# Attention products in pieces of 128 and 256 columns, ordered by the kernel's own clock model

## The chip, the cores and the metric

The kernel runs on one core of a Trainium2 chip. The time is that of one execution on the device, in microseconds (us). A comparison of two kernels is made from several rounds on the same chip. The engines are named as in the profile: PE is TensorE's matmul, PEld its loading of weights, ACT is ScalarE, DVE is VectorE, POOL is GpSimd, SP is SyncE.

## The reference

Two independent results stand side by side in the output, each 2048 x 576.

The first is a long convolution of a state-space model. For each of 576 channels, a kernel of 2048 taps is summed from 128 complex exponentials and convolved with the input; the reference does it by FFT.

The second is attention with 32 query heads of 18 columns and one shared key and value head:

```python
q = (x @ wq).reshape(B, S, H, Dh).transpose(0, 2, 1, 3)    # S = 2048, H = 32, Dh = 18
k = x @ wk
v = x @ wv
scores = einsum("bhqd,bkd->bhqk", q, k) * Dh ** -0.5
o = einsum("bhqk,bkd->bhqd", softmax(scores), v)
out = o.transpose(0, 2, 1, 3).reshape(B, S, H * Dh) @ wo
```

## The kernel before

**Attention.** The queries are cut into four chunks of 512 (`c`), the heads into eight groups of four (`g`), the keys into sixteen blocks of 128 (`kb`). For one chunk, group and block there are two score tiles (`j` = 0, 1) of two heads each, so the main loop (`main`, L963) runs over 4 x 8 x 16 x 2 = 1024 items, numbered `i`. Each item goes through three stations:

- `scores` (L720): two matmuls of 512 columns in half precision give a tile of 128 keys by 2 x 512 queries in PSUM. There are three such tiles (`NS` = 3), used in turn.
- `exponentials` (L734): one ACT instruction turns the tile into a tile P in SBUF. Eight P tiles exist (`NP` = 8).
- `product` (L1003): the product of P with V. The four heads of two neighbouring items stand side by side in four column strips of TensorE, so a product takes two items. It has 512 columns and is cut into two halves of `HN` = 256 columns, each with four matmuls, one per strip; an fp32 matmul appears as two instructions in the trace, so a half is 8 matmul records. The sum over the sixteen key blocks is kept in one PSUM bank, which DVE then copies out (`gather`).

**The side work.** The same PE and DVE also do the query projections (`qproj`, tiles named q), the output projection (`outproj`, `outproj_part`, op), and the whole convolution in twelve chunks of 48 channels (class `Conv`: tables and their products kg, transforms hu, lu, hk, lk, inverse iy). They share one PSUM bank, tag `f`. Their code is written as generators that yield before each piece: kind "p" for a piece on PE, "v" for one on DVE, "w" for a wait, "b" for a change of ACT's function table.

**What sets the order.** The program is emitted once, in one order for each engine, and the engines keep that order. The class `Clock` (L99) follows the time on each engine while the program is written: `K.t` is PE's time, `K.s[...]` the moments at which the score tiles come free, `turn` (L189) a cost for changing between scores and the rest. Between each three scores stands `fill(i)` (L1033). It computes `free`, the moment from which the next three scores can go without waiting for ACT, and `late`, which is `free` plus the allowance `SLACK` (L57). As long as `left = late - K.t` allows it, pieces are handed out in this order of preference: the convolution (`conv.go`, with `left + LET`), side work that is under way (`beside(left, False)`), new side work where the plan is behind (`behind_plan`, L988), a half product if one is ripe and `left > ROOM` (L1046), any side work. `beside` (L993) asks for `left - 0.43 > 0`; where a due time is nearer than `URGENT` steps (a step is two items) it adds `OVER` to `left`. Nothing more being ready, `K.t` moves on to the next event or to `free`, and the scores follow. Outside `fill`, products are forced when the eight P tiles would run out (`while (i - NP) // 2 >= behind // 2`).

`behind` counts the halves that have been given out, `ripe` (L1026) says when the next one can go. The other constants are allowances and paces of the same model: `PACE` is read in `lags` (L1627), which nothing calls; `RATE` holds the convolution's DVE work to so many us a step (L1606), `AHEAD` (L1609) limits how far DVE's queue is filled ahead of PE, `PATIENCE` is the number of steps that a table change waits, `FIRST` the earliest time of the first input transform, `PLAN` and `START` say how many side units should be done by a step, `CLEAR` how near a convolution piece must be to hold back new side work, `FEW` and `NEW` compare the number of items not yet multiplied.

Of the kernel before, what the change touches and what calls it, by code (L numbers as in the profile page):

```python
# [23 lines left out]
NCH = 4  # L24
CT = 512
KT = [(k * 128, 128) for k in range(5)]
HN = 256
DT = KT[:4] + [(512, 64)]
MT = [(0, 126), (126, 126), (252, 126), (378, 126), (504, 72)]
QT = [(0, 128), (128, 128), (256, 128), (384, 128), (512, 64)]  # L30
# [16 lines left out]
NP = 8  # L47


RATE = 6.724  # L50
PACE = 1.7672
AHEAD = 0.484
NAUG = 5
URGENT = 8.8421
HELD = 0
PATIENCE = 1
SLACK = 0.2043  # L57
FEW = 12
NEW = 3
LET = -0.1  # L60
PLAN = 0.629
START = 6.0
OVER = 0.6
CLEAR = 1.6188

LATE = {1: [0], 3: [1], 5: [2], 6: [3]}

# [10 lines left out]

HOP = 0.075
GRAIN = 128  # L80
FIRST = 20.4516
FETCH = 4.3
ROOM = 0.3889
INTO = 0.113
BACK = 0.104
EPS = 0.019


# [10 lines left out]
class Clock:  # L99
# [89 lines left out]
    def turn(self, mode):  # L189

        if mode != self.mode:
            self.t += INTO if mode else BACK
            self.mode = mode
# [157 lines left out]
class Stream:  # L351
# [3 lines left out]

    def __init__(self, gen, clock, ahead=AHEAD):
        self.gen, self.k, self.ahead = gen, clock, ahead
# [24 lines left out]
    def go(self, step, credit, lock=None):  # L382
# [4 lines left out]
        if self.kind == "p":  # L387
            ready = self.ready if self.holds else max(self.ready, k.fill)
            if credit <= 0 or k.t < ready - EPS or lock not in (None, self):
                return False  # L390
# [18 lines left out]
class Attention:  # L409
# [553 lines left out]
    def main(self, conv, flag):  # L963
        nc, K = self.nc, self.k
        conv.beside = lambda: self.o_left + self.q_left
        side = self.side_work
        K.reset(0.0, 0.7, 0.0)
        self.o_free = 0.0
        side.when = 0.0
        for st in conv.streams:  # L970
            st.when = 0.0
        prep = Stream(self.prepare(), K, 99.0)
        pairs = [(c, g, kb, j) for c in range(NCH) for g in range(8) for kb in range(16) for j in range(2)]
        def holder():
            return next((st for st in [side] + conv.streams if st.holds), None)

        def force(done):
            while not done():
                st = holder()
                (side if st is None else st).advance()  # L980
                self.fetch(self.group)

        def pump():

            while any(st.go(self.step, -1.0, holder()) for st in [x for x in (holder(),) if x] + [prep, side, conv]):
                pass

        def behind_plan():  # L988

            s = self.step  # L990
            return self.units < PLAN * s + START or self.due < 128 and self.due - s < 2 * self.q_left + 14

        def beside(left, new):  # L993

            if side.holds == new:
                return False
            if new and self.due < self.step + URGENT:
                left += OVER
            elif new and any(st.live and st.kind == "p" and st.ready < K.t + CLEAR for st in conv.streams):
                return False  # L1000
            return side.go(self.step, left - 0.43, holder())

        def product():  # L1003
            nonlocal o_ps, behind
            n, f = divmod(behind, 2)
            c, g, kb, _ = pairs[2 * n]
            if kb + f == 0:
                o_ps = self.ps_o.tile([P, CT], F32, tag="o", name=f"ops{c}_{g}")
            cs = slice(f * HN, f * HN + HN)
            for j in range(4):  # L1010
                nc.tensor.matmul(o_ps[32 * j:32 * j + 32, cs], self.v[:, kb, :], pts[2 * n + j // 2][:, j % 2, cs],
                                 start=(kb + f == 0), stop=(kb + f == 16), tile_position=(0, 32 * j))
            K.t = max(K.t, ripe())
            K.pe(0.434, o_ps)
            behind += 1
            if f == 0:
                return
            read[n] = K.t + 0.2
            if kb == 15 and (c, g) != (NCH - 1, 7):
                self.gather(c, g, o_ps)  # L1020
                if g == 7:
                    self.todo.append((c, range(5)))
                if c == NCH - 1 and g in LATE:
                    self.todo.append((c, LATE[g]))

        def ripe():  # L1026

            i = behind - behind % 2
            if i + 1 not in done:
                return 1e9  # L1030
            return max(done[i + 1] + 0.12 + HOP, self.o_free if pairs[i][2] == 0 and i == behind else 0.0)

        def fill(i):  # L1033

            free = max(K.s[(i + j) % NS] - 0.225 * j for j in range(NS)) - 0.113
            late = free + SLACK
            while True:
                pump()
                left = late - K.t
                if conv.go(self.step, left + LET, holder()):  # L1040
                    continue
                if i - behind < FEW and beside(left, False):
                    continue
                if i - behind < NEW and behind_plan() and beside(left, True):
                    continue
                if behind < len(pairs) and ripe() <= K.t + 0.02 and left > ROOM:  # L1046
                    product()
                    continue
                if beside(left, False) or beside(left, True):
                    continue  # L1050
                if K.t >= free:
                    return
                at = min((x for x in [free, ripe()] + [st.event() for st in [prep, side] + conv.streams] if x > K.t), default=free)
                K.t = min(max(at, K.t + 0.01), free)
                if K.t >= free - 0.01:
                    K.t = free
                    return
        o_ps, pts, done, read, behind = None, {}, {}, {}, 0
        for i, (c, g, kb, j) in enumerate(pairs):
            self.step = i // 2  # L1060
            if i == 120:
                self.load_wo()
            if i in (9, 18, 27):
                m = i // 9 + 1
                nc.vector.memset(self.wq[m][0:1, 0, 0:1], 0.0)
                self.load_wq(m)
            if (g, kb, j) == (0, 0, 0):
                self.od[c] = self.dr.tile([8 * P, CT], F32, tag="od", name=f"od{c}")
            if i >= 2 and i % NS == 0:
                fill(i)  # L1070
            force(lambda: 16 * c + 2 * g + j in self.ready)
            ps = self.scores(i, c, 2 * g + j, kb, 0.225)
            if i == 1:
                self.late_setup()
                self.second()
            if i == 2:
                self.values()
                self.maxima()
            while (i - NP) // 2 >= behind // 2:
                product()  # L1080
            pts[i] = self.exponentials(i, c, 2 * g + j, kb, *ps, read.get((i - NP) // 2, 0.0))
            done[i] = K.a
            if j == 0:
                continue
            self.group = (i + 1) // 32
            self.fetch(self.group)
            nxt = 16 * c + 2 * g + 3
            if kb >= 12 and nxt < 64:
                force(lambda: nxt in self.ready)
        while behind < len(pairs):  # L1090
            pump()
            product()

        while self.todo or self.busy or holder() or any(m == 0 for _, _, m in self.rest):
            if self.todo or self.busy:
                if prep.kind == "v":
                    K.t = max(K.t, prep.ready)
                prep.advance()
            else:
                (holder() or side).advance()  # L1100
        conv.drain()
        nc.vector.tensor_scalar(flag, self.ubound[0:1, :], UNIT * LIMIT / (2 * SCALE), None, op0=ALU.is_le)
        self.finish(NCH - 1, self.part, o_ps, self.w4, self.b4)
# [86 lines left out]
class Conv:  # L1190
# [374 lines left out]
    def inputs(self):  # L1565

        for k in range(NCK):
# [3 lines left out]
            if k == 0:  # L1571
                yield "v", FIRST, False
            ut = self.ut.pop(k)
# [31 lines left out]
    def go(self, step, credit, lock):  # L1605
        lag = step * RATE - self.work  # L1606
        if lag < -20.0:
            return False
        ahead = AHEAD + min(max(lag, 0.0) / 20.0, 1.0)  # L1609
        for st in self.streams:  # L1610

            if st.kind == "b":
                if st.asked < 0:
                    st.asked = step
                if self.hold is None:
                    if self.beside() >= 8 or step > st.asked + PATIENCE:
                        self.hold = step
# [9 lines left out]
    def lags(self, step):  # L1627
        return self.work < step * PACE and any(st.live and st.kind == "p" for st in self.streams)

# [119 lines left out]
```

## Time and profile before

| what | value |
|---|---|
| median of 3 runs | 1177.22 us (1175.84 to 1178.73) |
| the profiled execution | 1179.98 us |
| its span | 1178.1 us |
| granted TensorE clock, mean | 0.984 |
| matmul records on PE | 17974 |
| bytes moved by DMA | 123.84 MB, 105 GB/s |

Rows of groups in the profile read: line, engine, operation, output <- inputs, shapes, count; then busy us and the mean ns of one; then the idle time of the engine before them and what ended it. Many rows carry line 290, because a helper issues the matmuls; the tile names tell them apart (`s` scores, `ops` products). Rows of waits read: who waited <- for whom, us in total, times, the longest. Rows of the timeline read: start, length, engine, line, operation, tiles, shapes, count, and in brackets idle time before it. The end of a matmul is modelled, so neighbours overlap in the timeline and starts are the safer reading.

### The profile page before, as it was taken

What the parts mean: (1) busy time and instruction counts of PE and PEld (TensorE: products, weight loads), DVE (VectorE), ACT (ScalarE), POOL (GpSimd) and SP (SyncE); (2) the same over time, 40 slices, a digit from 0 to 9 for tenths busy, and PEclk for the clock granted to TensorE, in tenths of its full rate; (3) what the DMA queues carried; (4) which work ended last, traced back from release to release, by engine and by line L of the source; (5) the groups of instructions that cost most, each with busy time, mean ns of one, the idle gap of its engine ahead of it and who ended that gap; (6) DMA issues with size and microseconds to landing.
All of it is one profiled execution on the core that took longest, in us unless ns stands there. A gap on an engine that the chain in (4) does not pass through costs nothing. (4 is left out here: it accounts for less than half of the span.)

```text
span 1178.1 us, 41252 instructions
## 1 busy us (share of the span) xinstructions
PE 1109.0 (94%) x17974; PEld 536.5 (46%) x17974; DVE 923.4 (78%) x1645; ACT 1038.2 (88%) x1092; POOL 97.4 (8%) x151
## 2 busy tenths in 40 slices
PE   7999999899999898999898999899999999999897
PEld 1444444344544344444444444445445445444344
DVE  7776887987886795698897698895897988894643
ACT  5887999898999997899998899999989998998892
POOL 2001100201110000010111010000010200010100
PEclk9999999899999999999999999999999999999999
DMA  8332261524162523133434323343243252242421
GB/s 305 126 105 76 84 163 57 156 68 146 41 168 84 146 69 134 39 84 100 144 99 132 114 59 100 124 119 100 80 99 116 63 156 88 75 84 91 103 62 44
DMA packets 55021, 123.84 MB, mean 105 GB/s; under 512 B 7500, under 2 KB 24925, under 8 KB 53555
## 3 DMA queue, kind: packets, MB, share of 16 engines
q1 hardware_dynamic: 43571, 87.44, 21.6%
q0 software_dynamic: 10832, 33.27, 13.3%
q8 instruction: 143, 2.34, 0.8%
q10 hardware_dynamic: 432, 0.44, 0.1%
q14 instruction: 43, 0.35, 0.1%
HBM read 53.47 MB, written 41.46 MB: 81 GB/s over the span
## 5 line engine op out<-in xcount | busy, mean ns | idle before, releaser
L742 ACT ACTIVATE P<-s 128x1024 f32<-128x1024 f32 x992 | 941.8, 1028 | 102.3 <-PE s L290 94.5
L290 PE MATMUL ops<-P,v_sb 128*32 128x256 f32 x8192 | 550.4, 386 | 11.0 <-ACT P L742 6.2
L290 PEld LDWEIGHTS ops<-P,v_sb 128*32 128x32 f32 x8192 | 245.4, 110 | 224.3 <-issue 85.8
L290 PE MATMUL s<-aug,kaug 55*128 55x512 f16 x2048 | 301.0, 385 | 16.8 <-ACT P L742 9.7
L290 PEld LDWEIGHTS <-kaug 55*128 55x128 f16 x2048 | 91.5, 94 | 219.7 <-issue 175.3
L290 PE MATMUL q<-x,wq_sb 128*32 128x256 f32 x1360 | 88.9, 390 | 6.6 <-DVE ql L345 4.0
L290 PE MATMUL op<-wo_sb,oT 126*32 126x288 f32 (+1 forms) x1088 | 79.2, 415 | 7.3 <-DVE ob L329 4.4
L290 PEld LDWEIGHTS q<-x,wq_sb 128*32 128x32 f32 x1360 | 41.7, 112 | 43.1 <-issue 16.5
L325 DVE TENSOR_TENSOR tab<-tab,tt 128x576 f32<-128x576 f32 (+1 forms) x72 | 59.2, 822 | 1.9
L325 DVE TENSOR_TENSOR tab<-tab 128x576 f32<-128x576 f32 (+1 forms) x72 | 58.7, 816 | 0.0
L325 DVE TENSOR_TENSOR ks<-ks 128x384 f32<-128x384 f32 (+2 forms) x84 | 55.2, 669 | 1.7
L290 PEld LDWEIGHTS op<-wo_sb,oT 126*32 126x32 f32 (+1 forms) x1088 | 33.4, 111 | 42.0 <-issue 9.6
L275 POOL DMA_DIRECT2D qd<-qh x46 | 25.6, 569 | 308.9 <-DVE qh L333 308.9
L325 DVE TENSOR_TENSOR t<-us,ks 128x1728 f32<-128x1728 f32 (+2 forms) x36 | 47.2, 1346 | 0.0
L290 PE MATMUL kg<-tab 128*32 128x64 f32 x2304 | 42.2, 220 | 4.1 <-DVE tab L325 1.7
L290 PEld LDWEIGHTS kg<-tab 128*32 128x32 f32 x2304 | 37.2, 110 | 17.9 <-issue 3.8
L329 DVE COPY ob<-op 128x288 f32<-128x288 f32 x24 | 10.8, 452 | 43.4 <-PE op L290 42.9
L275 POOL DMA_DIRECT2D ks<-ks x12 | 10.9, 912 | 378.9 <-DVE ksb L329 254.8
L329 DVE COPY ksb<-kg 128x192 f32<-128x192 f32 x48 | 17.2, 359 | 30.4 <-PE kg L290 30.2
L325 DVE TENSOR_TENSOR acc<-acc 128x768 f32<-128x768 f32 (+1 forms) x48 | 40.3, 854 | 0.7
L740 ACT ACTIVATE P<-s,nb 128x1024 f32<-128x1024 f32 x32 | 33.2, 1116 | 6.2 <-PE s L290 6.1
L325 DVE TENSOR_TENSOR acc<-us,ks 128x768 f32<-128x768 f32 x36 | 33.1, 949 | 6.7 <-DMA ks<-ks 6.7
(356 smaller groups left out, 1086.1 us busy)
## 6 DMA issues: line engine op xcount, KB each, us to landing
park<-two SPq DMA_DIRECT2D x6, 1944.0 KB
acc<-t POOLq DMA_DIRECT2D x12, 864.0 KB, 6.6
od<-o SPq DMA_DIRECT2D x31, 256.0 KB
acc<-t POOLq DMA_DIRECT2D x12, 576.0 KB, 5.9
aug<-qd SPq DMA_DIRECT2D x124, 54.0 KB
u<-u SPq DMA_DIRECT2D x12, 384.0 KB
kd<-ksb SPq DMA_DIRECT2D x12, 384.0 KB
kt<-kd SPq DMA_DIRECT2D x48, 96.0 KB
```

The source lines that it names most:

```text
L275: return self.q.dma_start(out, src, **k)
L290: return self.e.matmul(out, w, x, **k)
L325: return self.v.tensor_tensor(out, a, b, **k)
L329: return self.v.tensor_copy(out, src)
L740: nc.scalar.activation(pt, ps, AF.Exp, scale=SCALE / UNIT ** 2, bias=self.nb)
L742: nc.scalar.activation(pt, ps, AF.Exp, scale=SCALE / UNIT ** 2)
```

## The change

Products may be handed out in quarters of 128 columns. `behind` counts quarters; `product` takes a size, two quarters by default, and one where `left` lies between the new limit `TIGHT` and `ROOM`. A piece that begins at the last quarter is a quarter in any case, and one that begins at the second quarter spans columns 128 to 384. Thirteen constants of the model change in the same edit. The computation is the same.

```diff
-HN = 256
+HN = 128
...
-RATE = 6.724
-PACE = 1.7672
-AHEAD = 0.484
+RATE = 7.6355
+PACE = 0.7665
+AHEAD = 0.3715
 NAUG = 5
-URGENT = 8.8421
+URGENT = 8.8475
 HELD = 0
-PATIENCE = 1
-SLACK = 0.2043
-FEW = 12
+PATIENCE = 0
+SLACK = 0.1334
+FEW = 11
 NEW = 3
-LET = -0.1
+LET = -0.0691
 PLAN = 0.629
-START = 6.0
-OVER = 0.6
-CLEAR = 1.6188
+START = 11.4238
+OVER = 0.8948
+CLEAR = 1.826
...
-FIRST = 20.4516
+FIRST = 23.1632
 FETCH = 4.3
-ROOM = 0.3889
+ROOM = 0.4379
 INTO = 0.113
 BACK = 0.104
+TIGHT = 0.1981
...
-        def product():
+        def product(size=2):
             nonlocal o_ps, behind
-            n, f = divmod(behind, 2)
+            n, f = divmod(behind, 4)
+            size = min(size, 4 - f)
...
-            cs = slice(f * HN, f * HN + HN)
+            cs = slice(f * HN, (f + size) * HN)
             for j in range(4):
                 nc.tensor.matmul(o_ps[32 * j:32 * j + 32, cs], self.v[:, kb, :], pts[2 * n + j // 2][:, j % 2, cs],
-                                 start=(kb + f == 0), stop=(kb + f == 16), tile_position=(0, 32 * j))
+                                 start=(kb + f == 0), stop=(kb == 15 and f + size == 4), tile_position=(0, 32 * j))
             K.t = max(K.t, ripe())
-            K.pe(0.434, o_ps)
-            behind += 1
-            if f == 0:
+            K.pe(0.217 * size, o_ps)
+            behind += size
+            if f + size < 4:
                 return
...
-            i = behind - behind % 2
+            i = 2 * (behind // 4)
...
-                if i - behind < FEW and beside(left, False):
+                if i - behind / 2 < FEW and beside(left, False):
                     continue
-                if i - behind < NEW and behind_plan() and beside(left, True):
+                if i - behind / 2 < NEW and behind_plan() and beside(left, True):
                     continue
-                if behind < len(pairs) and ripe() <= K.t + 0.02 and left > ROOM:
-                    product()
+                if behind < 2 * len(pairs) and ripe() <= K.t + 0.02 and left > TIGHT:
+                    product(2 if left > ROOM else 1)
                     continue
...
-            while (i - NP) // 2 >= behind // 2:
+            while (i - NP) // 2 >= behind // 4:
                 product()
...
-        while behind < len(pairs):
+        while behind < 2 * len(pairs):
```

More of the change, by code (lines that the diff above doesn't have):

```diff
@@ L1026, in ripe @@
         def ripe():
-            i = behind - behind % 2
+            i = 2 * (behind // 4)
             if i + 1 not in done:
                 return 1e9
-            return max(done[i + 1] + 0.12 + HOP, self.o_free if pairs[i][2] == 0 and i == behind else 0.0)
+            return max(done[i + 1] + 0.12 + HOP, self.o_free if pairs[i][2] == 0 and behind % 4 == 0 else 0.0)
         def fill(i):
```

## The prediction

> **What bounds the kernel now.** I read the page's totals and groups first, then the waits by engine, then the timeline of one quiet stretch for TensorE (PE) and for ScalarE (ACT). The totals and the three large groups:
>
> ```profile
> span 1178.1 us, 41252 instructions
> PE 1109.0 (94%) x17974; PEld 536.5 (46%) x17974; DVE 923.4 (78%) x1645; ACT 1038.2 (88%) x1092; POOL 97.4 (8%) x151
> ...
> L742 ACT ACTIVATE P<-s 128x1024 f32<-128x1024 f32 x992 | 941.8, 1028 | 102.3 <-PE s L290 94.5
> L290 PE MATMUL ops<-P,v_sb 128*32 128x256 f32 x8192 | 550.4, 386 | 11.0 <-ACT P L742 6.2
> ...
> L290 PE MATMUL s<-aug,kaug 55*128 55x512 f16 x2048 | 301.0, 385 | 16.8 <-ACT P L742 9.7
> ```
>
> ACT does little but exponentials, and stands idle for 102.3 us in front of them; nearly all of that, 94.5 us, ends when scores arrive from PE. PE is busy for 94%, but its ends are modelled, so it has at least the 69 us that are left and probably more. Neither engine alone fills the span. What is lost is lost in the hand-over, three scores at a time. The waits in both directions:
>
> ```profile
> ACT P L742 <- PE s L290: 94.5, 232, 3.7
> ...
> PE s L290 <- ACT P L742: 9.7, 26, 0.5
> PE ops L290 <- ACT P L742: 6.2, 7, 3.5
> ```
>
> ACT waits 232 times, 0.41 us each; PE waits visibly for ACT only 33 times, 15.9 us together. So PE comes late far oftener than it comes early. How late, and after what, the timeline shows; PE first, then ACT in the same stretch:
>
> ```profile
> 822.07 0.82 PE L290 MATMUL s<-aug,kaug 55*128 55x512 f16 x6
> 822.82 1.50 PE L290 MATMUL q<-x,wq_sb 128*32 128x256 f32 x24
> 824.14 1.05 PE L290 MATMUL ops<-P,v_sb 128*32 128x256 f32 x16
> 825.12 0.82 PE L290 MATMUL s<-aug,kaug 55*128 55x512 f16 x6
> 825.87 2.37 PE L290 MATMUL ops<-P,v_sb 128*32 128x256 f32 x40
> 828.17 0.82 PE L290 MATMUL s<-aug,kaug 55*128 55x512 f16 x6
> 828.92 0.64 PE L290 MATMUL ops<-P,v_sb 128*32 128x256 f32 x8
> 829.38 1.91 PE L290 MATMUL q<-x,wq_sb 128*32 128x256 f32 x32
> 831.22 0.82 PE L290 MATMUL s<-aug,kaug 55*128 55x512 f16 x6
> 831.97 0.64 PE L290 MATMUL q<-x,wq_sb 128*32 128x256 f32 x8
> 832.43 1.91 PE L290 MATMUL ops<-P,v_sb 128*32 128x256 f32 x32
> 834.27 0.82 PE L290 MATMUL s<-aug,kaug 55*128 55x512 f16 x6
> ```
>
> ```profile
> 825.61 2.86 ACT L742 ACTIVATE P<-s 128x1024 f32<-128x1024 f32 x3 [0.20 <-PE s L290]
> 828.66 2.86 ACT L742 ACTIVATE P<-s 128x1024 f32<-128x1024 f32 x3 [0.19 <-PE s L290]
> 831.71 2.86 ACT L742 ACTIVATE P<-s 128x1024 f32<-128x1024 f32 x3 [0.19 <-PE s L290]
> 834.76 5.61 ACT L742 ACTIVATE P<-s 128x1024 f32<-128x1024 f32 x6 [0.20 <-PE s L290]
> ```
>
> Read starts, since ends are modelled. Six score matmuls take 0.75 us until the next work starts (825.12 to 825.87). Forty matmuls, five half products, take 2.30 (825.87 to 828.17); sixteen before scores take 0.98 (824.14 to 825.12); the difference, 24 matmuls or three halves, is 1.32, so a half is 0.44, and about 0.11 of each stretch goes to the turn to scores. The period is 3.05 us (825.12 to 828.17), always five pieces of about 0.43 whatever they are. ACT needs 2.86 for its three exponentials and idles 0.19 to 0.20. Four pieces would make 2.62, and PE would wait for ACT; five make 3.05, and ACT waits for PE. The best number for ACT is four and a half: 0.75 + 0.11 + 4.5 x 0.44 = 2.84. That is the grain that the change alters.
>
> **The change part by part.** *The size of a piece.* A half is 8 matmuls of 256 columns, a quarter 8 of 128 (with a weight load each, as before). No row shows 128 columns in products; a finer one is there:
>
> ```profile
> 504.75 0.85 PE L290 MATMUL kg<-tab 128*32 128x64 f32 x48
> 505.54 0.82 PE L290 MATMUL s<-aug,kaug 55*128 55x512 f16 x6
> ```
>
> ```profile
> L290 PEld LDWEIGHTS kg<-tab 128*32 128x32 f32 x2304 | 37.2, 110 | 17.9 <-issue 3.8
> ```
>
> From its start to the scores is 0.79, less the 0.11 of the turn 0.68: 48 matmuls with 3072 columns, 0.22 ns a column; a half has 2048 columns in 0.44, 0.21 ns a column. So matmuls of 64 columns run at the rate of 256, with 110 ns loads hidden, and a quarter costs 0.21 by the half's rate and 0.23 by the kg row's. I take 0.22, half a half, with 0.01 as overhead of each added piece. A price below 0.21 is excluded, since the columns are the same. The Trainium skill speaks against this: its page "TensorE: Matmul & The Clock Gate", section "Back-to-back issue gap", gives about 81 ns per matmul of 128 columns in a stream of loads and matmuls, by which a quarter would take eight times that, 0.65 us as an estimate, more than a half, and the change would lose on every quarter. The trace disagrees: the kg row has 14 ns per matmul, loads included.
>
> *Where quarters come.* A half is started today while `left` is over 0.389, so by the kernel's own clock it ends at most 0.204 + 0.434 - 0.389 = 0.25 after the moment `free` at which scores could go, and the next choice leaves up to 0.389 - 0.204 = 0.185 before it unused. After the change, halves end at most 0.133 + 0.434 - 0.438 = 0.13 late, quarters 0.133 + 0.217 - 0.198 = 0.15 late, and at most 0.198 - 0.133 = 0.065 is left unused. The window for a quarter is 0.438 - 0.198 = 0.24 wide in a grid of 0.434: 55% of the fills that end with products. In the stretch above three of four fills end so (before the scores at 825.12, 828.17 and 834.27; the one before 831.22 ends with q); I take a little less, 60%, of the 341 fills (1024 scores, three at a time), so 341 x 0.6 x 0.55 = 113 quarters that end a fill, and about as many added pieces (a unit of four quarters then goes in three pieces). Products rise from 8192 matmuls to about 8192 + 8 x 113 = 9100, at 113 x 0.01 = **1.1 us** more PE time.
>
> *What that gains.* For ACT the upper bound is 113 x 0.19 = 21 us: the fifth piece becomes a quarter and the wait of 0.19 goes. But the other quarter is not gone; it must fit in a later fill. It is free only where PE waits for ACT today. Rows show 9.7 + 6.2 = 15.9 us of such waits; 55% of it is **8.7 us**. The lower bound is nothing. I take 8.7, which lies between, and nearer to the lower end because PE is the fuller engine. What is late next is PE itself: with full fills the scores wait for nothing but their turn.
>
> *Allowances for the other work.* `beside` starts a unit while `left` is over 0.43; with SLACK 0.071 smaller it stops that much earlier before `free`. Convolution pieces stop 0.071 - 0.031 = 0.04 earlier. Both leave less lateness and more room, which the quarters take; only where no product is ripe is PE idle for it. Of 341 fills at most a tenth (33 visible waits, above), at 0.04 to 0.07 each: **1 us** worse, between 0 and 2.3. For queries with a near due time the allowance OVER grows by 0.295, net of SLACK 0.22. Where it is used, scores come that much later; the row for a late query group:
>
> ```profile
> 839.05 1.50 PE L290 MATMUL q<-x,wq_sb 128*32 128x256 f32 x24
> 840.49 0.82 PE L290 MATMUL s<-aug,kaug 55*128 55x512 f16 x6
> ```
>
> ```profile
> 840.98 2.86 ACT L742 ACTIVATE P<-s 128x1024 f32<-128x1024 f32 x3 [0.61 <-PE s L290]
> ```
>
> This wait is 0.42 over the usual 0.19. START 5.4 units higher lets queries begin some 9 steps of two scores sooner, so fewer come due: I take 0, with both signs in the range. PACE is read only by a function that nothing calls, so it does nothing; nor does FEW, 12 to 11, because the ring of 8 P tiles forces products before the backlog reaches either. RATE holds the convolution back only where its VectorE work runs ahead of 6.7 us a step; 512 steps of that are over 3400 us, against 923.4 us of VectorE work in all, so it binds before and after about nowhere: 0. AHEAD shortens by 0.11 us the queue that VectorE is given: 0, hidden behind PE's products; where none is ripe it costs that 0.11 once. FIRST moves one transform 2.7 us later, the first of twelve chunks', with products at hand in its place: 0, or 2.7 if nothing else were ready. PATIENCE lets the table switch come a step sooner, with the same instructions on ACT: 0. No DMA is added or moved past another in any queue by the code; only the moments follow.
>
> **Sum.** -8.7 + 1.1 + 1 = -6.6 us. The profiled execution took 1179.98 (span 1178.1 and 1.9 around it), so 1173.4 for such a one. The median of the runs shown is 1177.22, 2.76 less: **1170.6 us**.
>
> **The rivals.** *Late queries* (slower). With OVER larger, query units start when up to 0.6 us over `free` instead of 0.37, and ACT waits as at 840.98. For it: the group
>
> ```profile
> L290 PE MATMUL q<-x,wq_sb 128*32 128x256 f32 x1360 | 88.9, 390 | 6.6 <-DVE ql L345 4.0
> ```
>
> is 170 units in some 17 tiles, and each tile has a due time. If two or three fills per tile use the allowance, 45 x 0.29 = 13 us are lost: 1177.2 - 6.6 + 13 = **1183.6**. It decides from 23 such fills on. Against it: START begins them sooner.
>
> *PE is full* (same). A quarter less in one fill is a quarter more in the next, ACT's wait of 0.19 turns up there, and the 15.9 us were waits at places where no product was ripe. The 94% speak for it; 1177.2 + 1.1 = **1178**. The same time comes if quarters are hardly used, because side work takes the room first, as q does in two of four fills above: then the matmul count stays under 8400.
>
> *A quarter as dear as a half* (slower): if the 110 ns load of each strip came ahead of its stream, every quarter would cost 0.22 more, 226 quarters 50 us: **1220**. The kg row speaks plainly against it. By the 81 ns that the Trainium skill's page "TensorE: Matmul & The Clock Gate" gives, section "Back-to-back issue gap", it would be 226 x 0.43 = 97 us, an estimate.
>
> **How the numbers follow.** Forecast 0.55; late queries 0.23; PE full or quarters unused 0.20; dear quarters 0.02. Differences under 0.3%, 3.5 us, can't be told from no change here. The forecast's own range runs from three quarters of ACT's upper bound, 1177.2 - 16 + 1 = 1162, to 1174. The range over all reaches 1160 to 1184, to take in late queries at their price; outside are more late queries than that, dear quarters, and a gain near ACT's 21 us. Faster 0.54, same 0.21, slower 0.25.
>
> **What would show it.** Right: a group of products with 128 columns in 8 x 100 to 8 x 300 matmuls, each eight 0.22 us after the one before; ACT's wait for scores clearly under 94.5 us; periods of 2.86 to 2.95 where 3.05 stands; PE's waits for ACT in front of scores and products near half of 15.9. Wrong: ACT's wait unchanged with PE's share up (PE full); ACT's waits of over 0.5 us after q more frequent (late queries); quarters 0.3 us or more apart; or fewer than 30 of them.

## The result, and the profile after

The changed kernel takes 1162.86 us (median of five, 1162.16 to 1167.64) against 1178.04 us (median of five, 1175.84 to 1180.47): a ratio of 0.9879, 95% interval 0.9854 to 0.9903. The profiled execution took 1167.64 us, 12.3 less than the one before. Its totals and large groups, from the page:

```profile
span 1165.9 us, 42886 instructions
PE 1102.5 (95%) x18790; PEld 563.4 (48%) x18790; DVE 924.4 (79%) x1649; ACT 1038.6 (89%) x1092; POOL 97.4 (8%) x151
...
L743 ACT ACTIVATE P<-s 128x1024 f32<-128x1024 f32 x992 | 942.0, 1027 | 91.3 <-PE s L291 87.3
...
L291 PE MATMUL s<-aug,kaug 55*128 55x512 f16 x2048 | 292.7, 381 | 11.3 <-ACT P L743 5.8
```

All lines stand one lower than before. The busy time of ACT, DVE and POOL is the same within 1 us; PE has 816 more matmul records (18790 for 17974). The groups with shapes kept apart show them:

```profile
L291 PE MATMUL ops<-P,v_sb 128*32 128x256 f32 x7376 | 501.1, 383 | 7.9 <-DVE o L330 5.7 <-ACT P L743 1.1 <-issue 0.8
...
L291 PE MATMUL ops<-P,v_sb 128*32 128x128 f32 x1632 | 82.7, 275 | 0.2 <-DVE o L330 0.2
```

That is 1632 / 8 = 204 quarters. The waits between PE and ACT, in the order who waited, for whom, us, times, longest:

```profile
ACT P L743 <- PE s L291: 87.3, 245, 5.2
```

```profile
PE s L291 <- ACT P L743: 5.8, 16, 0.5
...
PE ops L291 <- ACT P L743: 1.1, 5, 0.2
```

PE's waits for ACT fell from 15.9 to 6.9 us, ACT's for scores from 94.5 to 87.3. A stretch of the timeline, PE and then ACT:

```profile
805.64 0.40 PE L291 MATMUL ops<-P,v_sb 128*32 128x128 f32 x8
805.98 0.82 PE L291 MATMUL s<-aug,kaug 55*128 55x512 f16 x6
...
812.06 0.82 PE L291 MATMUL s<-aug,kaug 55*128 55x512 f16 x6
812.81 2.37 PE L291 MATMUL ops<-P,v_sb 128*32 128x256 f32 x40
815.11 0.82 PE L291 MATMUL s<-aug,kaug 55*128 55x512 f16 x6
```

```profile
806.49 5.67 ACT L743 ACTIVATE P<-s 128x1024 f32<-128x1024 f32 x6 [0.20 <-PE s L291]
812.55 2.86 ACT L743 ACTIVATE P<-s 128x1024 f32<-128x1024 f32 x3 [0.40 <-PE s L291]
815.60 2.85 ACT L743 ACTIVATE P<-s 128x1024 f32<-128x1024 f32 x3 [0.19 <-PE s L291]
```

A quarter before scores takes 0.34 to the next start, 0.11 of it the turn. But five halves in a row, 3.05 us from scores to scores (812.06 to 815.11), are still there, and so is ACT's idle time of 0.19 to 0.20 behind them. Where a quarter ends the fill, at 805.98, ACT idles 0.20 as well.

It helps to cut the span at the last exponential. The rows of the exponentials have their first and last start; before, then after:

```profile
L742 ACT ACTIVATE P<-s x992: 1014/1024/1112, 64.1 to 1156.0; 128x1024 f32<-128x1024 f32 x199
```

```profile
L743 ACT ACTIVATE P<-s x992: 1013/1025/1071, 66.1 to 1147.3; 128x1024 f32<-128x1024 f32 x199
```

The stretch of exponentials went from 1091.9 to 1081.2 us (-10.7), the end behind it from 22.1 to 18.6 (-3.5), and the beginning grew by 2.0: together -12.2.

### The profile page after: what moved, and what is told of

The parts are those of the page before. It is cut to its first block, busy times and chain, and to the rows that moved or that the text cites. A ratio compares the mean times of both kernels' runs of the same rounds, so it can differ in the third digit from the quotient of the medians.

```text
span 1165.9 us, 42886 instructions
## 1 busy us (share of the span) xinstructions
PE 1102.5 (95%) x18790; PEld 563.4 (48%) x18790; DVE 924.4 (79%) x1649; ACT 1038.6 (89%) x1092; POOL 97.4 (8%) x151
## 5 line engine op out<-in xcount | busy, mean ns | idle before, releaser
L743 ACT ACTIVATE P<-s 128x1024 f32<-128x1024 f32 x992 | 942.0, 1027 | 91.3 <-PE s L291 87.3
L291 PE MATMUL ops<-P,v_sb 128*32 128x256 f32 (+1 forms) x9008 | 550.2, 364 | 8.1 <-DVE o L330 6.0
L291 PEld LDWEIGHTS ops<-P,v_sb 128*32 128x32 f32 x9008 | 271.5, 110 | 218.5 <-issue 74.6
L291 PE MATMUL s<-aug,kaug 55*128 55x512 f16 x2048 | 292.7, 381 | 11.3 <-ACT P L743 5.8
L291 PEld LDWEIGHTS <-kaug 55*128 55x128 f16 x2048 | 95.0, 94 | 185.1 <-issue 137.6
L291 PE MATMUL op<-wo_sb,oT 126*32 126x288 f32 (+1 forms) x1120 | 85.4, 428 | 8.7 <-DVE ob L330 5.1
L291 PEld LDWEIGHTS op<-wo_sb,oT 126*32 126x32 f32 (+1 forms) x1120 | 35.3, 114 | 43.0 <-issue 10.2
L291 PEld LDWEIGHTS kg<-tab 128*32 128x32 f32 x2304 | 36.8, 112 | 23.9 <-issue 15.2
L334 DVE TENSOR_SCALAR qh<-q 128x256 f16<-128x256 f32 x34 | 14.1, 416 | 37.3 <-PE q L291 37.3
L326 DVE TENSOR_TENSOR us<-us 128x384 f32<-128x384 f32 (+1 forms) x60 | 37.1, 633 | 1.0
(356 smaller groups left out, 1076.7 us busy)
```

The source lines that it names most:

```text
L291: return self.e.matmul(out, w, x, **k)
L326: return self.v.tensor_tensor(out, a, b, **k)
L334: return self.v.tensor_scalar(out, src, *a, **k)
L743: nc.scalar.activation(pt, ps, AF.Exp, scale=SCALE / UNIT ** 2)
```

## The experiments

Seven of the thirteen retuned constants change nothing in this program. With RATE, PACE, URGENT, FEW, LET, START and OVER put back in the changed kernel, all at once, each engine's list of instructions is the same to the last one. They cannot have moved its time. (In e2 and e9 below, which have no quarters, the same seven do alter the order.) What is left are the quarters with TIGHT, and SLACK, ROOM, AHEAD, PATIENCE, CLEAR and FIRST.

This table has all runs; "stretch" and "end" are worked out as above, from the profiled execution. Each ratio is to executions of the kernel before in the same rounds (their medians lay at 1174.75 to 1178.04 us), so kernels of different rounds are compared by their ratios and not by their medians. "Waits" is the sum of ACT's waits for scores and products in front of exponentials (the rows of lines 742 and 740, after 743 and 741; 94.5 + 6.1 + 5.9 before).

| kernel | median us | ratio to before, 95% | stretch | end | waits |
|---|---|---|---|---|---|
| before | 1178.04 | 1 | 1091.9 | 22.1 | 106.5 |
| changed | 1162.86 | 0.9879 (0.9854 to 0.9903) | 1081.2 | 18.6 | 95.3 |
| e1, quarters only | 1177.94 | 1.0044 (1.0015 to 1.0073) | 1093.0 | 17.8 | 107.6 |
| e2, constants only | 1246.75 | 1.0636 (1.0591 to 1.068) | 1160.6 | 18.1 | 176.3 |
| e3, all quarters | 1199.93 | 1.0223 (1.0179 to 1.0268) | 1097.7 | 37.5 | 112.5 |
| e4, quarters and fill limits | 1175.70 | 1.0012 (0.9983 to 1.0042) | 1083.8 | 24.4 | 96.5 |
| e5, changed, ROOM 0.44 | 1170.73 | 0.9973 (0.995 to 0.9995) | 1082.5 | 21.9 | 97.7 |
| e6, before, SLACK 0.2053 | 1187.88 | 1.0136 (1.01 to 1.0172) | 1095.0 | 23.6 | 109.7 |
| e7, paces only | 1183.47 | 1.0069 (1.0043 to 1.0095) | 1097.0 | 24.1 | 111.2 |
| e8, changed, PATIENCE 1 | 1180.70 | 1.0056 (1.0031 to 1.0081) | 1076.7 | 40.5 | 89.7 |
| e9, halves, tight limits | 1216.27 | 1.0335 (1.0303 to 1.0368) | 1116.2 | 28.7 | 128.6 |
| e10, changed, AHEAD 0.38 | 1185.66 | 1.0076 (1.0046 to 1.0106) | 1094.2 | 24.5 | 107.4 |
| e11, before, ROOM 0.395 | 1173.28 | 0.9973 (0.9948 to 0.9999) | 1084.7 | 22.2 | 99.5 |
| e12, e8 with the last sums first | 1178.23 | 1.0018 (0.9991 to 1.0046) | 1075.9 | 37.2 | 90.3 |

Three theories stand against each other. A: the finer grain brings the gain. B: the new constants bring it by what they are. C: the order of the instructions is drawn by lot, in the sense that any edit which shifts one choice of the clock model gives a different order from there on, and orders differ in time.

**e1, the quarters only.** The changed code with the constants of before:

```diff
-SLACK = 0.1334
+SLACK = 0.2043
-ROOM = 0.4379
+ROOM = 0.3889
...
```

> The code for quarters with TIGHT 0.1981, and every other constant as before (SLACK 0.2043, ROOM 0.3889 and so on). Theory A, the grain: quarters by themselves close the ends of the fills, so most of the 1.2% comes already, a ratio to before of 0.988 to 0.993. Theory B, the constants: the gain is that of the allowances and paces, so this stays at 0.997 to 1.003. Theory C, the order is drawn by lot: any edit that reshuffles the order moves the time by up to 1% either way, and this lies anywhere from 0.99 to 1.01 without a tie to the count of quarters.

It came out slower by 0.4%, a little outside B's interval too. There are 120 quarters, at the price forecast, and no gain:

```profile
L291 PE MATMUL ops<-P,v_sb 128*32 128x128 f32 x960 | 48.5, 275 | 0.7 <-DVE o L330 0.7
```

Theory A as written falls.

**e2, the constants only.** `TIGHT = 0.4379` in the changed kernel, so that no quarter is chosen.

> The changed kernel with TIGHT raised to ROOM (0.4379), so that no quarter is chosen; all new constants stay. Theory A: no gain, rather a small loss, since a fill may now leave up to 0.438 - 0.133 = 0.30 us before the scores unused: 0.997 to 1.01. Theory B: 0.986 to 0.991, as the full change. Theory C: anywhere from 0.99 to 1.01.

6.4% slower: far beyond what each theory gave. The new constants without quarters are harmful, so B as written falls too. Where it goes is shown with e9.

**e3, all quarters.**

```diff
-                    product(2 if left > ROOM else 1)
+                    product(1)
```

> The changed kernel with every chosen product a quarter, also where there is room for a half: some 900 added pieces. If a quarter is half of a half plus 0.003 to 0.01 us, this adds 3 to 9 us to the changed kernel at most: 0.985 to 0.998 of before. If an added piece cost 0.05 us, 45 us come on top: over 1.02. If a quarter were as dear as a half, 900 x 0.22 = 200 us: 1.15 or more.

2.2% over before and 3.5% over the changed kernel. By the total alone this is the case of 0.05 us for an added piece, but the price of a piece isn't the reason: inside a run of quarters each starts 0.218 us after the one before, as these rows of e3 show for ten of them with the turn (829.41 - 827.09 = 2.32; (2.32 - 0.11) / 10 = 0.22):

```profile
827.09 2.39 PE L291 MATMUL ops<-P,v_sb 128*32 128x128 f32 x80
829.41 0.82 PE L291 MATMUL s<-aug,kaug 55*128 55x512 f16 x6
```

In 35 us of span more than the changed kernel's, 19 lie behind the last exponential (37.5 against 18.6) and 16 in the stretch. A quarter isn't dear; an order with many of them isn't good.

**e4, quarters and the limits of the fill.** As e1, but with SLACK, ROOM and LET as changed.

> Quarters and the limits of the fill as changed (SLACK, ROOM, TIGHT, LET), all other constants as before (AHEAD, PATIENCE, CLEAR, FIRST, RATE, START, OVER, URGENT, FEW). Theory A: the whole gain or nearly, 0.985 to 0.991, and not more than 0.3% from the changed kernel. Theory B with the paces as its cause: 0.995 to 1.003. Theory C: more than 0.4% from both the changed kernel and the quarters alone, to either side.

The ratio is 1.0012: not A's, and 1.3% from the changed kernel; it lies where B put it with the paces as cause, which e7 and e8 take up. C's condition isn't met either: from e1 it is only 0.3%. But the stretch of exponentials is 1083.8 us, close to the changed kernel's, with waits of 96.5; its end of 24.4 us is longer by 5.8.

**e5 and e6, empty edits.** `ROOM = 0.44` for 0.4379 in the changed kernel, `SLACK = 0.2053` for 0.2043 in the kernel before.

> The changed kernel with ROOM 0.44 in place of 0.4379. Two thousandths of a microsecond in one allowance mean nothing by any mechanism, but they put the rest of the order on another course (the first difference is followed by thousands). Theory B, the constants matter by what they are: 0.986 to 0.991 of before, as the changed kernel. Theory C, the order is drawn by lot: it leaves that interval, most likely upwards, 0.992 to 1.005, since the changed kernel's order is one good draw among many.

> The kernel before with SLACK 0.2053 in place of 0.2043, as empty an edit as the last, on the other side. Theory B: 0.998 to 1.002. Theory C: 0.99 to 1.012, outside 0.997 to 1.003 more likely than not.

Both left B's intervals: 0.9% up on the changed kernel's side, 1.4% up on the other, which is a little over C's 1.012 as well. ACT's row of e6, to be held beside 94.5 before, has more waiting for the same work:

```profile
ACT P L742 <- PE s L290: 98.2, 222, 11.3
```

So an edit that means nothing moves this kernel by as much as the change did. That is C, shown.

**e7, the paces only.** The kernel before with AHEAD, PATIENCE, CLEAR and FIRST as changed.

> The kernel before, halves alone and its own limits of the fill, with AHEAD, PATIENCE, CLEAR and FIRST as changed. Theory B with the paces as cause: 0.986 to 0.992, the whole gain without quarters. Theory A', that quarters and paces are needed together: 0.997 to 1.003. Theory C: anywhere from 0.99 to 1.01.

0.7% slower. The paces bring no gain of their own with halves, so B is left with nothing but combinations.

**e8, PATIENCE 1 in the changed kernel.**

> The changed kernel with PATIENCE 1 as before, so a change of ACT's table waits one step longer. Theory B with this constant as cause: back to 0.997 to 1.002. If patience does nothing: 0.986 to 0.991. Theory C: it leaves the changed kernel's interval by 0.3% or more, like the empty edit of ROOM, since it reshuffles the order too.

1.8% above the changed kernel, although its stretch of exponentials is the shortest but one of all (1076.7 us):

```profile
L743 ACT ACTIVATE P<-s x992: 1012/1026/1072, 65.4 to 1142.1; 128x1024 f32<-128x1024 f32 x199
```

All is lost behind the last exponential: 40.5 us for 18.6. The timeline of PE there:

```profile
1153.78 1.51 PE L291 MATMUL iy<-acc,dft_sb 128*32 128x192 f32 x16 [9.50 <-DVE acc L326]
...
1157.24 2.51 PE L291 MATMUL iy<-w,dft_sb 128*32 128x192 f32 x32 [0.67 <-DVE out L330]
...
1159.57 3.57 PE L291 MATMUL fin<-wo_sb,oT 126*32 126x288 f32 x56
```

The convolution's last inverse transform, which in the changed kernel ended ahead of the last exponentials, comes here after them, and PE stands 9.5 us before it with the attention's last sums (`fin`) queued behind. The trace also grants only half of TensorE's clock for 10.2 us there, from 1149.1 us on.

**e9, halves with tight limits.** `TIGHT = ROOM = 0.318` in the changed kernel: a half may start as late as before, the limits for the other work are the tight ones.

> The changed kernel without chosen quarters (TIGHT = ROOM), with ROOM at 0.318, so that a half starts up to 0.185 us ahead of the free moment, as before, while SLACK 0.1334 and all else are as changed: the tighter limits for the side work alone, halves as they were. Judged by the last exponential's start, since the end is another matter. Theory D, quarters and tight limits are needed together: last exponential at 1153 to 1163, as in the three orders with halves and old limits (1155.9 to 1161.2), ACT's waits for scores 100 to 115 us. Theory B', the tight limits for the side work are the cause: 1140 to 1149, as in the four orders with quarters and tight limits, waits 88 to 98 us.

Neither: 3.4% slower, last exponential at 1178.4. The rows of ACT's waits say where:

```profile
ACT P L743 <- PE s L291: 89.4, 222, 5.2
ACT P L743 <- PE ops L291: 34.7, 20, 8.4
```

The wait for scores is lower than before (94.5), but ACT waits 34.7 us for products, where the kernel before has

```profile
ACT P L742 <- PE ops L290: 5.9, 9, 1.4
```

and e2 has 36.1: a P tile is to be written anew and the product that reads it hasn't run. It is not that products alone pile up. The longest such wait of e2, 17.47 us, has this ahead of it on PE, with neither scores nor products between the rows from 785.51 to 803.41:

```profile
785.51 2.64 PE L291 MATMUL op<-wo_sb,oT 126*32 126x288 f32 x40
...
795.15 2.37 PE L291 MATMUL q<-x,wq_sb 128*32 128x256 f32 x40 [0.58 <-DVE ob L330]
798.61 2.37 PE L291 MATMUL q<-x,wq_sb 128*32 128x256 f32 x40 [1.10 <-DVE ql L346]
803.17 0.31 PE L291 MATMUL up<-aw,all 128*32 128x8 f32 x16 [2.19 <-DVE aw L334]
803.41 0.39 PE L291 MATMUL s<-aug,kaug 55*128 55x512 f16 x2
```

```profile
804.90 5.83 ACT L743 ACTIVATE P<-s 128x1024 f32<-128x1024 f32 x6 [17.47 <-PE ops L291]
```

The query projections had fallen so far behind that `main` forced them (`force`, `self.ready`; `up` is a step of them) between two scores, one piece after the other waiting for DVE. In e9 the four longest waits for products stand behind late queries too, 22.1 of the 34.7 us: 8.45, 5.86 and 3.53 behind such projections, 4.26 where scores waited for the transfer of the queries. That the tight limits leave too little room for the side work when no quarter fills the rest fits this, but it is argued: SLACK alone with halves was not run, and e9 differs from the kernel before in the other constants as well. What is shown is that the new constants cost 3.4% and 6.4% without quarters.

**e10 and e11, two more nearly empty edits.** `AHEAD = 0.38` for 0.3715 in the changed kernel, `ROOM = 0.395` for 0.3889 in the kernel before. Theory D was what A had become: quarters with tight limits shorten the stretch, the end is a separate lot.

> The changed kernel with AHEAD 0.38 in place of 0.3715, one more near-empty edit that puts the order on another course. Theory D, quarters with tight limits shorten the stretch up to the last exponential in any order: last exponential at 1139 to 1150, ACT's waits under 98 us; what follows the last exponential is open, 18 to 40 us, and decides the total. Theory C, all is by lot: last exponential anywhere from 1139 to 1162.

> The kernel before with ROOM 0.395 in place of 0.3889, a near-empty edit. Theory D: last exponential at 1154 to 1162, ACT's waits over 105 us, and 22 us or more behind it. Theory C: anywhere from 1139 to 1162.

Both missed theory D's numbers for the last exponential:

```profile
L743 ACT ACTIVATE P<-s x992: 1015/1025/1106, 64.5 to 1158.7; 128x1024 f32<-128x1024 f32 x199
```

```profile
L742 ACT ACTIVATE P<-s x992: 1012/1025/1104, 64.0 to 1148.7; 128x1024 f32<-128x1024 f32 x199
```

The first is e10, later than the kernel before; the second is e11, about as early as the changed kernel, with halves alone. ACT's waits missed too (107.4 and 99.5 in the table). D in its strict form falls. As a tendency it stays possible: five orders with quarters and tight limits (changed, e4, e5, e8, e10; e12 is e8 with another end) have a mean stretch of 1083.7 us, four with halves and the old limits (before, e6, e7, e11) 1092.2; the difference of 8.5 has a standard error of 4.0 from the spread of the two groups. In ratios the groups stand at 1.000 and 1.004, with 0.005 as the error of the difference.

**e12, the last sums first.** In e8, `self.finish(...)` stands ahead of `conv.drain()`.

> The changed kernel with PATIENCE 1 (1180.7 us, of which some 40 us lie behind the last exponential) with the attention's last sums issued ahead of the convolution's last pieces, in place of behind them. If the 40 us are long because PE stood 9.5 us before the last chunk's inverse transform and the last sums queued behind it, they shrink by 9 to 15 us, to 25 to 31, the total to 1166 to 1172, and the stretch before stays as it was within 2 us. If they are long for another reason (more sums left over), nothing moves by more than 3 us.

1178.23 us, ratio 1.0018 (0.9991 to 1.0046); the end shrank from 40.5 to 37.2 us, 3.3 and not 9 to 15. PE's row shows where it went:

```profile
1164.99 1.51 PE L291 MATMUL iy<-acc,dft_sb 128*32 128x192 f32 x16 [6.52 <-issue]
```

The last sums went ahead, but the transform now begins at 1165.0 in place of 1153.8. The edit also put DVE's adds for the sums ahead of DVE's last steps of the convolution; that these delayed it is likely, and wasn't tried by itself. That PE's order alone made the end long is not borne out.

## Why the prediction was right, and where its steps were not

The time fell, inside the range; the gain was 15.2 us in the medians and 12.3 in the profiled executions, for 6.6 forecast. That it fell by that much is in good part luck: near-empty edits of the two kernels moved the time by -0.3% to +2.0%, and the changed kernel's order is the fastest of the fourteen timed. The pieces and their waits moved much as forecast, but the step from them to the time is not borne out.

**The price of a quarter** was right. From the start of one piece to that of the next, within a run of products, the median is 0.432 us for a half and 0.218 for a quarter: 2 x 0.218 - 0.432 = 0.004 for an added piece, where 0.01 was taken. The kg row was the right one to go by. Dear quarters are excluded.

**The count** was right: 204 quarters for 226, 9008 matmul records for 9100.

**The term of the gain**, 55% of PE's 15.9 us of waits, gave 8.7; the waits fell by 9.0. In this order the step holds to the number. It is not the cause of the time, though: e8 has 13.8 us of these waits (7.8 + 6.0) and a shorter stretch of exponentials. What goes with the stretch in the table is ACT's waiting, 95.3 for 106.5 in the changed kernel. And that did not fall where quarters were to help. One late half makes ACT wait at most some 0.63 us (0.19 + 0.44). Sorted by length in the traces, ACT's idle times in front of the 992 exponentials that are shorter than 0.7 us add up to 58.5 us before and 62.8 after (102.3 and 91.3 in all); in the other three orders with halves and old limits they are 56.9 to 62.2, in the other four with quarters and tight limits 58.3 to 61.4. The whole fall is in the longer ones, 43.6 to 28.4 us, which no single late half makes.

**"The best number for ACT is four and a half"** was wrong, and with it the upper bound of 21 us. The 0.19 to 0.20 us behind five halves are not the lateness of the fifth. The clock model puts them there: `free` lies 0.563 us (0.45 + 0.113) ahead of the release of the third tile, the first exponential can start 0.579 (0.113 + 0.225 + 0.166 + 0.075) after it, and the release is counted 0.195 (0.12 + 0.075) after the last exponential's end, so 0.21 remain when nothing is late. This is argued from the code; the rows of after, 0.20 where a quarter ended the fill in time, agree. So periods of 2.86 to 2.95 did not come: from one full group of six score matmuls to the next, 14 of 323 lie between 2.85 and 2.97 us after the change, 17 of 314 before. What became rarer are late ones, from 3.09 to 4 us: 80, 123 before.

**"Both leave less lateness and more room, which the quarters take"** was right about the pair, though nothing in the prediction said how much hung on it. It priced tight limits at 1 us. Without quarters the new constants, of which they are a part, cost 3.4% and 6.4% (e9, e2); quarters without them bring nothing (e1).

**The zeros** for AHEAD, PATIENCE, CLEAR and FIRST failed, and in a way that the prediction had no term for. Against the changed kernel, PATIENCE put back costs 1.8%, AHEAD moved by 0.0085 costs 2.0%, and ROOM moved by 0.0021 costs 0.9%. No mechanism of these sizes hangs on them; each puts the planner on another course. The zeros for RATE, PACE, FEW, START and OVER were right because they change no instruction here, which also left the rival of the late queries without a place in the changed kernel; queries did come late in e2 and e9, by another way. (That rival's price was too high by its own figures: from 0.374 to 0.598 us over `free` is 0.22 a fill and not 0.29, so 10 us and not 13.) *PE is full* did not happen in the changed kernel: ACT's wait fell with PE's share up by one point.

How much of the 1.2% belongs to finer pieces cannot be settled from these orders. The same-signed evidence is the stretch (8.5 us, error 4.0), the counter-evidence e10 and e11, and the short waits that did not shrink. The lot for the end behind the last exponential, 18 to 41 us in the kernels with quarters, is wider than that.

## What to carry to other kernels

Where a program's order comes from a planner that follows a clock, first move a constant by an amount that means nothing and time that: here it gave -0.3% to +1.4% on the kernel before and up to +2.0% on the changed one, so a gain of 1% says little about the idea behind it. Read such a kernel in parts (the stretch in which the two bound engines alternate, and the end behind it), since one part can win while the other loses more. Where a finer piece comes with tighter limits, try the pair and each alone: here the pieces alone brought nothing and the constants alone did harm. And look at the waits that the idea is meant to shorten, sorted by length, before the time is credited to it.

## What the runs showed of the hardware

Matmuls of 128 columns in four column strips ran at the rate of those of 256: 0.218 us for eight records, weight loads of 110 ns included and hidden.

The time of one and the same program goes with the granted clock of TensorE. Of the 72 executions of the kernel before with a clock on record, the fastest took 1166.14 us at a mean clock of 0.995, the slowest 1183.35 at 0.983. Over all executions of all kernels, each about its own mean, 0.01 of clock goes with 9.8 us. The trace of the kernel before grants either the whole clock or half of it: half in nine stretches, some 37 us in all, for example 752.4 to 755.8 us, and half of 37 us is the 0.016 that its mean lacks. The Trainium skill, page "TensorE: Matmul & The Clock Gate", section "Terms", puts the penalty of throttled time at that time multiplied by (1 - K/N); with half the clock granted, 0.01 of the mean over 1176 us is 23.5 us of such time and by the rule 11.8 us lost, as an estimate. The runs agree within a fifth: a little less is lost than the rule gives, perhaps because some of that time falls where PE waits anyway; that was not tried. Orders differ in it as well: the changed kernel's five executions had 0.988 to 0.993, e2's six 0.963 to 0.973. Brought to one clock of 0.988 with that slope, the changed kernel would take 1166.5 and the one before 1176.2, so about 10 us are left. Most of the rest of the 15 is that the first five executions of the kernel before lay above the mean of the 72, 1175.0 us. The clock is not independent of the order, though: in e9 two of the half-clock stretches begin at 872.7 and 1070.7, right behind PE's waits among forced queries, so part of what an order costs shows as clock.
